# Performer attention and two feed-forward layers: slopes by a sign per feature, five smaller staging buffers, weight units spread over more steps

## The chip, the cores and the metric

The kernel runs on one core of a Trainium2 chip. The metric is the time of one execution on the device in microseconds (us), the median of several runs.

Five engines work beside each other, each in the order of its own instructions, and wait for one another by semaphores: TensorE (PE in the profile; its weight loads are PEld), VectorE (DVE), ScalarE (ACT), GpSimd (POOL) and SyncE (SP), which here only issues transfers (DMA). Products land in PSUM, and DVE or ACT read them from there.

## The reference, cut to what matters

```python
# attention: q, k, v are (4, 8, 576, 64), omega is (128, 64)
h = x @ omega.T - sum(x*x)/2;  phi = exp(h - max(h)) / sqrt(128)      # for scaled q and k
num = phi(q) @ (phi(k).T @ v);  den = phi(q) @ sum(phi(k)) + 1e-6
x = (num / den)                                # as (2304 tokens, 512)
# layer 0 ("moe")
h = x @ w_in                                   # (2304, 2048)
g = np.maximum(h, 0.0) + alpha * np.minimum(h, 0.0)   # one slope alpha per feature, 0 to 0.3
x = g @ w_out                                  # (2304, 512)
# layer 1 ("moe2")
r = np.maximum(x @ w_in2, 0.0)
out = (r * r) @ w_out2
```

All inputs are float32, and so is the output.

## The kernel before

**Numbers in two parts.** TensorE multiplies in a rounded float32 (F32R in the code). Each operand is split: ACT rounds it (the high part), DVE subtracts the rounded from the raw (the low part, the remainder), and a product is three matmuls: high by high, high by low, low by high. `xh`, `xl` are the parts of the inputs, `gh`, `gl` those of the features, and the weights w hold both parts side by side.

**Stages.** Attention comes first (to about 145 us). Then layer 0 runs over three blocks of 768 tokens; in a block, eight turns each take one pair p of feature chunks of 128. Block 0 multiplies plainly (`plain`, eight steps a turn). Blocks 1 and 2 use a scheme of Strassen's kind with seven products of halves (`pair`, seven steps a turn, each one product of six matmuls of 384 columns). In PSUM two tiles a and b collect the products; ACT copies a to s (line 816), and DVE adds s to b (`plus`, line 821), which gives a quarter c of the features. Between the products, TensorE does the second multiplication (`mm2`, line 886) of the pair before, into y, in ten parts handed out by `FILL`. A turn of blocks 1 and 2 has 42 matmuls of products and 48 of `mm2`, 90 in all. At the end of a block y is copied out of PSUM (`evacuate`, line 904).

**The slopes** (`activate`, lines 740 to 762). For each quarter ACT makes n = relu(-c) and r = relu(c); when both halves of a chunk are there, DVE makes r = n * (-alpha) + r over 768 columns (line 754), ACT rounds it to gh (line 757), and DVE takes the remainder gl (line 760). These three are not issued at once: `catch_up` and `round_up` put each a step later on its engine than the one before.

**The weights of layer 1.** The inputs' weights arrive as float32 pairs of words, which have to be put together again: GpSimd loads 128 x 512 of them (512 KB, line 113), ACT scales two words (lines 123, 126), DVE shifts and merges (130, 133), GpSimd adds (135) into the tile `wf1`. DVE then makes four sums of weights (line 149), ACT rounds all eight pieces into staging tiles (line 196), DVE puts the remainders beside them (line 199), and SP writes the tiles to DRAM (`keep`, line 202, and `keep3`, line 223), from where layer 1 reads them later. One such run over 1792 KB of result is a unit; layer 1 has 16 of them (two kinds, `cast1` and `cast3`), made in blocks 1 and 2 of layer 0, eight in each.

**Staging and order.** There are two staging tiles, ma (three pieces, 768 KB) and ms (four pieces, 1024 KB), used by every unit in turn. `plan_unit` (line 287) lays a unit out on ten plan steps: casts into ma at 5 and 7, remainders at 6 and 8, write of ma at 8; casts into ms at 10 and 11, remainders at 11 and 13, write of ms at 13. Line 959 says how far the plan has to be at each of TensorE's 56 steps of a block: in block 1 it is spread over 44 steps from step 5 on, in block 2 over 46 from step 3 on. The work of the plan is issued on ACT, DVE, GpSimd and SP between the work of the steps, and each engine keeps to that order.

**Next block.** `NEXT` (line 403) lists the steps at which the inputs of the next block are prepared: four differences on DVE (line 386), seven roundings on ACT (393) and seven remainders on DVE (396), most of them from step 50 of a block to step 2 of the next.

SP also reads the weights of the next pair from DRAM into a ring of two (line 368): per turn 2 x 896 KB for the products and 2 x 512 KB for `mm2`.

Of the kernel before, what the change touches and what calls it, by code (L numbers as in the profile page):

```python
# [18 lines left out]
P = 128  # L19
# [35 lines left out]
def tile_performer_moe(ctx, tc, qt, kt, qn, kn, vn, omt, w1i, w1o, al, w2i, w2o, out):  # L55
# [8 lines left out]
    al_sb = const.tile([P, NF], F32, name="al_sb")  # L64
    x = const.tile([P, BLOCKS, KC, NB], F32, name="x")
# [90 lines left out]
    def made():  # L156
# [28 lines left out]
        def first(key, u, a0, a1):  # L185

            layer, p = key
            if layer == 0:
                return ring[p % 2][0][:, u, a0:a1]
            return tiles["ma"][:, u, a0 - A22:a1 - A22] if a1 <= S1 else tiles["ms"][:, u, a0 - S1:a1 - S1]  # L190
# [10 lines left out]
        def keep(key, which, at, tile, queue=nc.sync):  # L201
            queue.dma_start(out=kept[key][which][:, :, at].bitcast(F32), in_=tile.bitcast(F32))

            if at in (0, slice(0, 7), slice(3, 7)):
                done.add((key, which))
# [3 lines left out]
        def third(a0, a1):  # L209
            n, a = ("ma", 0) if a1 <= 3 else ("ms", 4)  # L210
            t = tiles[n].rearrange("p u n q -> p (u n q)").rearrange("p (n u q) -> p n u q", u=2, q=QW)
            return t[:, a0 - a:a1 - a]
# [74 lines left out]
        def plan_unit(n, base):  # L287
# [7 lines left out]
            if n1:  # L295
                cast, rest, keeps = (lambda *r: cast1(n1, *r)), (lambda *r: rest1(n1, *r)), [
                    lambda: keep(n1, 0, slice(0, 3), tiles["ma"]), lambda: keep(n1, 0, slice(3, 7), tiles["ms"])]
                first_, second_ = (A11, S1), (A22, A11)
            else:
                cast, rest, keeps = cast3, rest3, [lambda: keep3(n2[1], 0, 3), lambda: keep3(n2[1], 4, 8)]  # L300
                first_, second_ = (0, 2), (2, 3)
            put(-1 if n not in ENDS else 0, lambda: used[n, *a].scale_high())
# [119 lines left out]
    def attention():  # L422
        with ExitStack() as ac:
# [235 lines left out]
            for i in range(NT):  # L659
# [7 lines left out]
                if i == 8:  # L667
                    nc.vector.tensor_scalar(out=al_sb, in0=al_sb, scalar1=-1.0, scalar2=None, op0=ALU.mult)
# [61 lines left out]
    def features(layer, p):  # L730
# [9 lines left out]
        def activate(i, l, c, psum=False):  # L740

            ts = slice(l * HB, (l + 1) * HB)
            f = 2 * p + i
            if i not in halves:
                halves[i] = [new("r", 3, NB), new("n", 2, NB), 0]
            r, n = halves[i][:2]
            halves[i][2] += 1
            nc.scalar.activation(out=n[:, ts], in_=c, func=AF.Relu, scale=-1.0)
            nc.scalar.activation(out=r[:, ts], in_=c, func=AF.Relu)  # L749
            if halves[i][2] < 2:  # L750
                return

            def slope():
# [8 lines left out]
            behind[0].append((slope, high, low))  # L762

        def square(i, l, c, psum=False):

            to = g[i, l, p // 4][:, p % 4]
            if psum:
                r = new("r", 3, NB)[:, :HB]
                nc.scalar.activation(out=r, in_=c, func=AF.Relu)
# [16 lines left out]
            behind[0].append((power, high, low))  # L786

        return gh, gl, square if layer else activate

    def plain(p):  # L790

        w = ring[p % 2][0]
        gh, gl, activate = features(0, p)
# [481 lines left out]
```

## Time and profile before

| | |
|---|---|
| median of 3 runs | 905.99 us (902.18 to 906.78) |
| the profiled execution | 901.07 us, its span 899.0 us |
| granted TensorE clock, mean | 0.997 |
| busy: PE, PEld | 881.9 us (98%), 834.8 us (93%) |
| busy: DVE, ACT, POOL | 673.4 us (75%), 522.6 us (58%), 166.2 us (18%) |
| DMA | 228.81 MB, mean 255 GB/s |

The span runs from the first to the last instruction of the profiled execution. Busy time of a matmul includes its way through the array, so that neighbours overlap; how many matmuls pass in a stretch tells more than PE's busy share. In the lists of instructions a row has the line of the kernel, the engine, the operation, what it writes and reads, its shape and count, then busy time in us and mean ns of one, then the idle time before it and who ended it.

### The profile page before, as it was taken

How to read it: one execution, taken by the hardware profiler on the slowest of the kernel's cores; microseconds unless marked ns; L12 is line 12 of the kernel's file. 1: busy time of each engine (PE TensorE's matmuls, PEld its weight loads, DVE VectorE, ACT ScalarE, POOL GpSimd, SP SyncE). 2: the span in 40 equal slices, each digit the busy share in tenths (PEclk: the TensorE clock that was granted, in tenths of full speed). 3: DMA queues.
4: the chain of work that ended last, by engine and by line, in shares of the span. 5: the costliest groups of instructions: out<-in, count | busy, mean ns of one | idle time of the engine just before them, and what ended most of it. 6: DMA issues, size and time to landing. Idle time of an engine off the chain costs nothing.

```text
span 899.0 us, 18473 instructions
## 1 busy us (share of the span) xinstructions
PE 881.9 (98%) x7328; PEld 834.8 (93%) x7328; DVE 673.4 (75%) x1077; ACT 522.6 (58%) x1109; POOL 166.2 (18%) x192
## 2 busy tenths in 40 slices
PE   9999999999999999999999999999999999999998
PEld 7998889999998888898898999999999999999998
DVE  5868987998986887877788974668855688657674
ACT  6889886777676666667676753334523245333432
POOL 6642322444412322202232100000000000000000
PEclk9999999999999999999999999999999999999999
DMA  7644316898836999927999975767697686876763
GB/s 272 196 139 144 120 30 219 293 303 284 291 141 227 348 399 375 337 92 291 393 348 366 369 266 168 249 249 264 235 309 250 205 322 251 268 259 228 297 249 135
DMA packets 82293, 228.81 MB, mean 255 GB/s; under 512 B 6176, under 2 KB 16800, under 8 KB 77216
## 3 DMA queue, kind: packets, MB, share of 16 engines
q1 hardware_dynamic: 72640, 192.21, 59.7%
q0 software_dynamic: 9216, 33.56, 11.2%
q10 hardware_dynamic: 352, 1.87, 0.6%
q8 instruction: 58, 0.95, 0.4%
q14 instruction: 27, 0.22, 0.1%
HBM read 170.47 MB, written 57.15 MB: 253 GB/s over the span
## 4 chain that ended last, share of the span: by engine, by line
PE 52%; DMA 2%; DVE 2%; ACT 1%; issue 0%; ACTq 0%; DVEq 0%
PE h L717 15%; PE sumb L717 10%; PE suma L1075 9%; PE sumc L1075 8%; PE y L886 7%; PE sumb L1075 3%; DMA k<-ms 2%; DVE r L754 0%; PE h L1075 0%; DVE wf L149 0%; DVE ma L199 0%; ACT x L123 0%; DVE gl L760 0%; DVE c L821 0%; DVE t L130 0%
## 5 line engine op out<-in xcount | busy, mean ns | idle before, releaser
L717 PE MATMUL h<-xh,w 128*128 128x384 f32 x1040 | 296.6, 338 | 6.2 <-ACT s L816 6.2
L717 PEld LDWEIGHTS h<-xh,w 128*128 128x128 f32 x1040 | 191.5, 188 | 10.5 <-ACT s L816 8.0
L886 PE MATMUL y<-gh,w 128*128 128x512 f32 (+1 forms) x768 | 176.9, 339 | 5.2 <-ACT gh L757 5.0
L717 PE MATMUL h<-xl,w 128*128 128x384 f32 x520 | 175.2, 337 | 0.2 <-DVE xl L396 0.2
L886 PEld LDWEIGHTS y<-gh,w 128*128 128x128 f32 x768 | 131.7, 189 | 18.2 <-ACT gh L757 6.8
L135 POOL TENSOR_TENSOR wf<-x 128x512 int32<-128x512 int32 x64 | 81.9, 1280 | 240.5 <-issue 43.5
L1089 ACT CAST gh<-g 128x768 fp32r<-128x768 f32 x72 | 56.6, 833 | 81.0 <-PE suma L1075 38.9
L886 PE MATMUL y<-gl,w 128*128 128x512 f32 (+1 forms) x384 | 103.6, 338 | 0.0
L717 PEld LDWEIGHTS h<-xl,w 128*128 128x128 f32 x520 | 98.0, 188 | 3.2 <-DVE xl L396 0.6
L717 PE MATMUL sumb<-xh,w 128*128 128x384 f32 x336 | 91.2, 335 | 0.0
L1091 DVE TENSOR_TENSOR gl<-g,gh 128x768 fp32r<-128x768 f32 x72 | 65.8, 955 | 32.2 <-PE suma L1075 17.2
L886 PEld LDWEIGHTS y<-gl,w 128*128 128x128 f32 x384 | 67.5, 188 | 9.2
L717 PEld LDWEIGHTS sumb<-xh,w 128*128 128x128 f32 x336 | 61.4, 188 | 0.2 <-ACT s L1021 0.2
L1075 PE MATMUL sumc<-w,gh 128*128 128x256 f32 x416 | 61.3, 283 | 0.0
L499 DVE TENSOR_REDUCE mx<-h 128x8 f32<-128x1024 f32 x36 | 44.0, 1223 | 21.9 <-PE h L486 21.4
L754 DVE SCALAR_TENSOR_TENSOR r<-n,al_sb,r 128x768 f32<-128x768 f32 x48 | 55.9, 1164 | 1.4 <-ACT r L749 1.4
L1075 PEld LDWEIGHTS sumc<-w,gh 128*128 128x128 f32 x416 | 56.5, 192 | 0.0
L717 PE MATMUL sumb<-xl,w 128*128 128x384 f32 x168 | 56.2, 335 | 0.0
L1075 PE MATMUL suma<-w,gh 128*128 128x256 f32 x432 | 54.8, 283 | 0.0
L760 DVE TENSOR_TENSOR gl<-r,gh 128x768 fp32r<-128x768 f32 x48 | 53.4, 1116 | 0.9 <-ACT gh L757 0.9
L1075 PEld LDWEIGHTS suma<-w,gh 128*128 128x128 f32 x432 | 53.1, 192 | 0.0
L821 DVE TENSOR_TENSOR c<-h,s 128x384 f32<-128x384 f32 x51 | 28.2, 553 | 30.6 <-PE h L717 17.8
(112 smaller groups left out, 1554.5 us busy)
## 6 DMA issues: line engine op xcount, KB each, us to landing
w<-k SPq DMA_DIRECT2D x99, 512.0 KB, 5.2
w<-k SPq DMA_DIRECT2D x39, 1024.0 KB, 4.9
w<-k SPq DMA_DIRECT2D x26, 896.0 KB, 9.0
k<-ms SPq DMA_DIRECT2D x16, 1024.0 KB, 7.8
k<-w SPq DMA_DIRECT2D x7, 1792.0 KB, 7.8
k<-ma SPq DMA_DIRECT2D x16, 768.0 KB, 7.0
x<-in_w1i POOLq DMA_DIRECT2D x16, 512.0 KB, 4.1
x<-in_w1o POOLq DMA_DIRECT2D x16, 512.0 KB, 5.3
```

The costliest lines, as they stand in the source:

```text
L135: nc.gpsimd.tensor_tensor(out=self.out.bitcast(I32), in0=self.high, in1=self.low, op=ALU.add)
L499: nc.vector.reduce_max(out=mx, in_=pj, axis=AX.X)
L717: nc.tensor.matmul(out, w[:, u, a, cs], tiles[v, b][:, kc], start=start and kc == 0 and j == 0, stop=stop and kc == 1 and j == 2, skip_gro ...
L754: nc.vector.scalar_tensor_tensor(out=r, in0=n, scalar=al_sb[:, f:f + 1], in1=r, op0=ALU.mult, op1=ALU.add)
L760: nc.vector.tensor_tensor(out=gl[:, i], in0=r, in1=gh[:, i].bitcast(F32), op=ALU.subtract)
L821: nc.vector.tensor_tensor(out=c, in0=b, in1=s, op=ALU.add)
L886: nc.tensor.matmul(y[a0 // 512][:, a0 % 512:a0 % 512 + a1 - a0], u[:, i, c * P:(c + 1) * P], v[:, i, ts], start=first and j == 0 and a0 % ...
L1075: nc.tensor.matmul(to[c], (l if v == 2 else h)[:, r, c * P:(c + 1) * P], w[:, rr, v % 2], start=fresh and rr == 0 and v == 0 and (c != 1 o ...
L1089: nc.scalar.copy(out=h[:, r], in_=f[:, r])
L1091: nc.vector.tensor_tensor(out=l[:, r], in0=f[:, r], in1=h[:, r].bitcast(F32), op=ALU.subtract)
```

## The change

Three things are changed. First, the slopes: a table `sg_sb` holds a sign per feature, -1 where alpha is over 1 and +1 elsewhere. ACT's copy s and the quarter read straight from PSUM are scaled by the sign, DVE's sum becomes b * sign + s in one operation, the slope becomes max(c * alpha, c), and rounding and remainder multiply by the sign again. The relus are gone. In layer 1 the code is arranged anew; its operations stay.

Second, the staging: instead of ma and ms there are a tile for a single piece and a ring of four for two pieces each, the fourth being `wf2`, which is free by then. Each cast takes its own tile (`take`), and each remainder is followed by its own write, four per unit.

Third, line 959 (now 1004) spreads the units over 50 steps in block 1 and 49 in block 2.

```diff
+    sg_sb = const.tile([P, NF], F32, name="sg_sb")
...
+        def take(a0, a1):
+            if a1 - a0 == 1:
+                slots[a0] = tiles["single"]
+            else:
+                slots[a0] = tiles["double"][taken[0] % 4]
+                taken[0] += 1
...
+            def staging(a0, a1):
+                def begin():
+                    take(a0, a1)
+                    cast(a0, a1)
+                def end():
+                    rest(a0, a1)
+                    save(a0, a1)
+                return begin, end
+            (c1, r1), (c2, r2), (c3, r3), (c4, r4) = (staging(*at) for at in (first_, second_, (S1, S3), (S3, 8)))
...
-            put(5, lambda: merge(used[n, *b]), lambda: cast(*first_))
-            put(6, lambda: rest(*first_))
-            put(7, lambda: cast(*second_), lambda: sums((1, 2), not n1))
-            put(8, lambda: rest(*second_), keeps[0])
+            put(5, lambda: merge(used[n, *b]), c1)
+            put(6, r1)
+            put(7, c2, lambda: sums((1, 2), not n1))
+            put(8, r2)
             put(9, lambda: sums((3, 4), not n1))
-            put(10, lambda: cast(S1, S3))
-            put(11, lambda: cast(S3, 8), lambda: rest(S1, S3))
-            put(13, lambda: rest(S3, 8), keeps[1])
+            put(10, c3)
+            put(11, c4, r3)
+            put(13, r4)
...
-                    nc.vector.tensor_scalar(out=al_sb, in0=al_sb, scalar1=-1.0, scalar2=None, op0=ALU.mult)
+                    nc.vector.tensor_scalar(out=sg_sb, in0=al_sb, scalar1=1.0, scalar2=-2.0, op0=ALU.is_gt, op1=ALU.mult)
+                    nc.vector.tensor_scalar(out=sg_sb, in0=sg_sb, scalar1=1.0, scalar2=None, op0=ALU.add)
...
-            nc.scalar.activation(out=n[:, ts], in_=c, func=AF.Relu, scale=-1.0)
-            nc.scalar.activation(out=r[:, ts], in_=c, func=AF.Relu)
...
+            if s is None:
+                scaled(c[:, ts], b, i)
+            else:
+                nc.vector.scalar_tensor_tensor(out=c[:, ts], in0=b, scalar=sign, in1=s, op0=ALU.mult, op1=ALU.add)
...
-                nc.vector.scalar_tensor_tensor(out=r, in0=n, scalar=al_sb[:, f:f + 1], in1=r, op0=ALU.mult, op1=ALU.add)
+                nc.vector.scalar_tensor_tensor(out=c, in0=c, scalar=slope, in1=c, op0=ALU.mult, op1=ALU.max)
...
-                nc.scalar.copy(out=gh[:, i], in_=r)
+                scaled(gh[:, i], c, i)
...
-                nc.vector.tensor_tensor(out=gl[:, i], in0=r, in1=gh[:, i].bitcast(F32), op=ALU.subtract)
+                nc.vector.scalar_tensor_tensor(
+                    out=gl[:, i], in0=c, scalar=sign, in1=gh[:, i].bitcast(F32), op0=ALU.mult, op1=ALU.subtract)
...
-    for n, a in (("ma", 3), ("ms", 4)):
-        tiles[n] = mr.tile([P, 2, a, QW], F32R, name=n)
+    tiles["single"] = mr.tile([P, 2 * QW], F32R, name="ma")
+    tiles["double"] = [mr.tile([P, 4 * QW], F32R, name=f"ms{j}") for j in range(3)]
+    tiles["double"].append(tiles["wf2"].rearrange("p i n -> p (i n)").bitcast(F32R))
...
-                upto(end_of(ENDS[k - 1]) + (end_of(ENDS[k]) - end_of(ENDS[k - 1])) * (turn * 7 + m - (0, 5, 3)[k]) // (0, 44, 46)[k],
+                upto(end_of(ENDS[k - 1]) + (end_of(ENDS[k]) - end_of(ENDS[k - 1])) * (turn * 7 + m - (0, 5, 3)[k]) // (0, 50, 49)[k],
```

On ACT, in the middle of a block, before: the casts into staging (ma, ms), the copies s that TensorE waits for, and the relus n and r.

```order
L196 CAST ma<-wf_98 128x256
L816 COPY s<-h 128x384
L123 ACTIVATE x<-x 128x512
L196 CAST ms<-wf_98 128x512
L126 ACTIVATE x<-x 128x512
L196 CAST ms<-wf_98 128x512
L816 COPY s<-h 128x384
L748 ACTIVATE n<-c 128x384
L749 ACTIVATE r<-c 128x384
```

The same place of a unit on ACT after the change:

```order
L212 CAST ma<-wf_99 128x256
L771 ACTIVATE gh<-c,sg_sb 128x768
L771 ACTIVATE s<-h,sg_sb 128x384
L125 ACTIVATE x<-x 128x512
L212 CAST ms_2690<-wf_99 128x512
L128 ACTIVATE x<-x 128x512
L212 CAST ms_2691<-wf_99 128x512
L771 ACTIVATE s<-h,sg_sb 128x384
L125 ACTIVATE x<-x 128x512
L771 ACTIVATE c<-h,sg_sb 128x384
```

The casts still stand ahead of a copy s, but each has a tile of its own and no relus follow.

On SP's queue, where the first units of block 1 are written (k<-) between the reads of weights (w<-), before:

```order
L202 DMA k_1_0_72<-ma 256x1x768
L368 DMA w_1_2696<-k_5_85 128x2x512
L368 DMA w_0_100<-k_0_4_68 128x1792
L368 DMA w_1_2696<-k_5_85 128x2x512
L202 DMA k_1_0_72<-ms 256x1x1024
```

and after the change:

```order
L218 DMA k_1_0_73<-ms_2689 256x1x512
L218 DMA k_1_0_73<-ma 256x1x256
L396 DMA w_1_2695<-k_5_86 128x2x512
L396 DMA w_0_101<-k_0_4_69 128x1792
L218 DMA k_1_0_73<-ms_2690 256x1x512
L396 DMA w_1_2695<-k_5_86 128x2x512
L218 DMA k_1_0_73<-ms_2691 256x1x512
```

Two writes of a unit became four smaller ones, from four tiles.

On DVE in the last turn of block 1, where the remainders xl of the next block's inputs are made, before:

```order
L821 TENSOR_TENSOR c<-h,s 128x384
L760 TENSOR_TENSOR gl<-r,gh 128x768 x2
L396 TENSOR_TENSOR xl_1358<-x,xh_1357 128x768
L396 TENSOR_TENSOR xl_1360<-x,xh_1359 128x768
L821 TENSOR_TENSOR c<-h,s 128x384
L396 TENSOR_TENSOR xl_2685<-tb,xh_2684 128x768
L396 TENSOR_TENSOR xl_2683<-ta,xh_2682 128x768
```

and after the change:

```order
L795 SCALAR_TENSOR_TENSOR gl<-c,sg_sb,gh 128x768
L135 SCALAR_TENSOR_TENSOR x<-x,t 128x512
L424 TENSOR_TENSOR xl_1360<-x,xh_1359 128x768
L215 TENSOR_TENSOR ms_2689<-wf_99,ms_2689 128x512
L132 TENSOR_SCALAR t<-x 128x512
L424 TENSOR_TENSOR xl_1362<-x,xh_1361 128x768
L784 SCALAR_TENSOR_TENSOR c<-h,sg_sb,s 128x384
L135 SCALAR_TENSOR_TENSOR x<-x,t 128x512
L424 TENSOR_TENSOR xl_2682<-tb,xh_2681 128x768
L215 TENSOR_TENSOR ms_2690<-wf_99,ms_2690 128x2x256
```

Weight work (t, x, ms) now stands between these remainders, where the plan had ended before.

## Rows read from the trace of the kernel before

**Rows 1.** Busy time by stretch: start:end, us, engines (x instructions), PEclk, DMA share, GB/s

```profile
150.00:260.00 110.00, 110.00 (x630) 102.97 (x630) 99.36 (x141) 81.86 (x153) 43.40 (x46) 1.00 0.80 273
270.00:480.00 210.00, 198.63 (x1111) 182.20 (x1110) 162.33 (x263) 142.65 (x282) 50.48 (x56) 0.99 0.85 315
300.00:360.00 60.00, 55.96 (x314) 50.80 (x314) 46.98 (x80) 39.41 (x80) 15.27 (x16) 1.00 1.00 380
380.00:396.00 16.00, 15.69 (x90) 14.36 (x89) 13.07 (x19) 10.42 (x20) 0.30 (x1) 1.00 0.39 132
450.00:455.00 5.00, 5.00 (x23) 4.70 (x22) 4.97 (x8) 3.82 (x8) 1.90 (x2) 0.66 1.02 415
480.00:510.00 30.00, 30.00 (x172) 27.61 (x171) 27.96 (x46) 21.93 (x44) 8.54 (x8) 1.00 0.99 381
```

**Rows 2.** Whom PE waited for, whole span: us in total, times, longest us

```profile
PE h L717 <- ACT s L816: 6.2, 5, 1.7
PE y L886 <- ACT gh L757: 5.0, 4, 2.0
PE t L480 <- DVE pick L455: 1.2, 1, 1.2
PE h L486 <- ACT e L511: 0.4, 1, 0.4
PE h L717 <- DVE xl L396: 0.2, 1, 0.2
```

**Rows 3.** Timeline of ACT and PE, 372 to 376: start, us, instruction, [idle before, releaser]

```profile
372.75 0.62 ACT L196 CAST ms<-wf 128x512 fp32r<-128x512 f32 x1 [3.54 <-DMA k<-ms]
...
374.87 0.45 PE L717 MATMUL h<-xh,w 128*128 128x384 f32 x1 [1.59 <-ACT s L816]
```

**Rows 4.** Who waited for whom, all engines, whole span

```profile
ACT ms L196 <- DMA k<-ms: 17.1, 7, 4.0
```

**Rows 5.** Timeline of PE behind the start of block 2

```profile
415.50 0.96 PE L886 MATMUL y<-gh,w 128*128 128x512 f32 x4 [0.84 <-ACT gh L757]
```

**Rows 6.** DMA issues: count, KB each, median us from issue to landing

```profile
k<-ms SPq DMA_DIRECT2D x16, 1024.0 KB, 7.8
...
k<-ma SPq DMA_DIRECT2D x16, 768.0 KB, 7.0
```

**Rows 7.** Instructions of ACT, 276 to 545 us

```profile
L757 ACT CAST gh<-r 128x768 fp32r<-128x768 f32 x32 | 26.7, 833 | 1.8 <-DVE r L754 1.6
...
L748 ACT ACTIVATE n<-c 128x384 f32<-128x384 f32 x46 | 24.2, 526 | 33.9 <-DVE c L821 33.9
...
L816 ACT COPY s<-h 128x384 f32<-128x384 f32 x48 | 22.7, 473 | 9.6 <-PE h L717 9.1
```

**Rows 8.** Instructions of ACT by shape, to 276 and from 276 us

```profile
L511 ACT ACTIVATE e<-h,nb 128x128 f32<-128x128 f32 x144 | 39.1, 384 | 13.0 <-DVE nb L506 13.0
...
L904 ACT COPY x<-y 128x256 f32<-128x256 f32 x4 | 1.5, 372 | 0.6 <-DVE x L904 0.6
```

**Rows 9.** Instructions of DVE, 276 to 545 us

```profile
L754 DVE SCALAR_TENSOR_TENSOR r<-n,al_sb,r 128x768 f32<-128x768 f32 x32 | 34.2, 1068 | 0.0
L760 DVE TENSOR_TENSOR gl<-r,gh 128x768 fp32r<-128x768 f32 x32 | 33.1, 1040 | 0.0
L821 DVE TENSOR_TENSOR c<-h,s 128x384 f32<-128x384 f32 x49 | 27.1, 554 | 29.7 <-PE h L717 17.8 <-ACT s L816 11.5
...
L199 DVE TENSOR_TENSOR ms<-wf,ms 128x512 fp32r<-128x512 f32 x32 | 26.1, 816 | 12.2 <-ACT ms L196 12.2
L149 DVE TENSOR_TENSOR wf<-wf 128x256 f32<-128x256 f32 x64 | 25.5, 419 | 2.4 <-POOL wf L135 1.9
...
L133 DVE SCALAR_TENSOR_TENSOR x<-x,t 128x512 int32<-128x512 int32 x32 | 22.0, 687 | 0.3
L199 DVE TENSOR_TENSOR ma<-wf,ma 128x512 fp32r<-128x512 f32 (+1 forms) x32 | 21.8, 681 | 8.5 <-ACT ma L196 8.5
...
L130 DVE TENSOR_SCALAR t<-x 128x512 int32<-128x512 int32 x32 | 14.6, 456 | 5.5 <-ACT x L123 5.3
```

More of the change, by code (lines that the diff above doesn't have):

```diff
@@ L738, in features, with scaled, activate, bend @@
             parts(p)
[L740 removed]
+        def scaled(to, of, i):
+            nc.scalar.mul(out=to, in_=of, mul=sg_sb[:, 2 * p + i:2 * p + i + 1])
+        def activate(i, l, b, s=None):
             ts = slice(l * HB, (l + 1) * HB)
[L743 removed]
+            sign, slope = (t[:, 2 * p + i:2 * p + i + 1] for t in (sg_sb, al_sb))
             if i not in halves:
[L745 to L754 removed]
+                halves[i] = [new("c", 4, NB), 0]
+            c = halves[i][0]
+            halves[i][1] += 1
+            if s is None:
+                scaled(c[:, ts], b, i)
+            else:
+                nc.vector.scalar_tensor_tensor(out=c[:, ts], in0=b, scalar=sign, in1=s, op0=ALU.mult, op1=ALU.add)
+            if halves[i][1] < 2:
+                return None
+            def bend():
+                nc.vector.scalar_tensor_tensor(out=c, in0=c, scalar=slope, in1=c, op0=ALU.mult, op1=ALU.max)
@@ L766, in square, with plain_copy @@
+            return bend, high, low
+        def plain_copy(to, of, i):
+            nc.scalar.copy(out=to, in_=of)
+        def square(i, l, b, s=None):
             to = g[i, l, p // 4][:, p % 4]
+            c = new("c", 4, NB)[:, :HB]
+            psum = s is None
             if psum:
-                r = new("r", 3, NB)[:, :HB]
-                nc.scalar.activation(out=r, in_=c, func=AF.Relu)
+                r = c
+                nc.scalar.activation(out=r, in_=b, func=AF.Relu)
+            else:
+                nc.vector.tensor_tensor(out=c, in0=b, in1=s, op=ALU.add)
@@ L784, in low @@
                                             op=ALU.subtract)
-            behind[0].append((power, high, low))
-        return gh, gl, square if layer else activate
+            return power, high, low
+        return (gh, gl, square, plain_copy) if layer else (gh, gl, activate, scaled)
     def plain(p):
         w = ring[p % 2][0]
-        gh, gl, activate = features(0, p)
+        gh, gl, activate, _ = features(0, p)
         for n, (i, l) in enumerate(((1, 0), (0, 0), (1, 1), (0, 1))):
@@ L806, in pair @@
         w = ring[p % 2][0]
-        gh, gl, activate = features(layer, p)
+        gh, gl, activate, moved = features(layer, p)
         a, b = (mp["ph"].tile([P, 512], F32, name="h")[:, :HB] for _ in range(2))
@@ L812, in product, with copied @@
             multiply(out, w, *PRODUCTS[n], start, True)
-        def copied():
+        def copied(i):
             s = new("s", 2)
-            nc.scalar.copy(out=s, in_=a)
+            moved(s, a, i)
             return s
-        def plus(s):
-            c = new("c", 3)
-            nc.vector.tensor_tensor(out=c, in0=b, in1=s, op=ALU.add)
-            return c
         product(a, 1, True)
-        s = copied()
+        s = copied(0)
         catch_up()
@@ L828, in pair @@
         product(b, 2, True)
-        c = plus(s)
+        one = activate(0, 0, b, s)
         catch_up()
-        activate(0, 0, c)
+        then(one)
         yield
         product(a, 6)
-        s6 = copied()
+        s6 = copied(0)
         catch_up()
@@ L840, in pair @@
         product(a, 7)
-        s7 = copied()
-        c = plus(s7)
+        s7 = copied(1)
+        one = activate(1, 1, b, s7)
         catch_up()
-        activate(1, 1, c)
+        then(one)
         yield
@@ L847, in pair @@
         catch_up()
-        activate(1, 0, a, True)
+        then(activate(1, 0, a))
         yield
         product(b, 3)
-        c = plus(s6)
+        one = activate(0, 1, b, s6)
         catch_up()
-        activate(0, 1, c)
+        then(one)
         yield gh, gl
@@ L866, in catch_up, with then @@
         behind[:] = [], made_, rounded
+    def then(one):
+        if one:
+            behind[0].append(one)
     def round_up():
@@ L1021, in copied @@
             nc.scalar.copy(out=kept_[n], in_=a)
-        def plus(n):
-            c = new("c", 3)
-            nc.vector.tensor_tensor(out=c, in0=b, in1=kept_[n], op=ALU.add)
-            return c
         def step(n):
@@ L1033, in step @@
                 copied(n)
-            c = plus({2: 1, 7: 7, 3: 6}[n]) if n in (2, 7, 3) else None
+            at = {2: (0, 0, 1), 7: (1, 1, 7), 3: (0, 1, 6)}.get(n)
+            one = activate(*at[:2], b, kept_[at[2]]) if at else None
             if n != 3:
                 catch_up()
-            if n == 4:
-                activate(1, 0, a, True)
-            elif c is not None:
-                activate(*{2: (0, 0), 7: (1, 1), 3: (0, 1)}[n], c)
+            then(activate(1, 0, a) if n == 4 else one)
             if p + 2 < NPAIR and n in GROUPS:
```

23 lines of the change are left out of this document (11 added, 12 removed).

## The prediction

> **What bounds the kernel now.** I read the stage windows first, then who waits for whom, then the instruction lists around the waits. TensorE is busy nearly everywhere; the reader is to see where it is not. In block 0 of layer 0 it has no gap [rows 1], and at the end of block 2 it passes 172 matmuls in 30 us, 5.73 per us, so that a turn of 90 matmuls takes 15.7 us. From 270 to 480 us, which is blocks 1 and 2 with the making of layer 1's weights, there are 1111 matmuls in 210 us; at 5.73 they would take 194 us. By busy time the loss there is 11.4 us, and the 5 us with 23 matmuls at a granted clock of 0.66 (a mix of the 1.2 and 2.4 GHz levels, right behind the longest wait of 2.0 us) add about 1 us. I take 14 us as the loss, between 12.4 and 16. The waits say who it is: TensorE waits for ACT alone, 6.2 us for the copy s and 5.0 us for the rounding gh [rows 2]. ACT is late for a reason of its own: its cast into the staging tile ms stood 3.54 us until an earlier write out of ms had landed, the copy s was queued behind it (the order shown with the change), and TensorE stood 1.59 us for s [rows 3]. There are six such waits of TensorE from 304 to 477 us, 1.2 to 2.0 us each, 9.2 us together. ACT's waits for ms are 17.1 us in all [rows 4]. The remaining 2 us are of the kind of [rows 5]: at the start of a block ACT is simply behind, and gh comes 0.84 us late.
>
> **Deeper staging, slower weight plan.** A unit is 10 plan steps. In block 1 eight units lie on 44 of the 56 TensorE steps now, so that a unit takes 5.5 steps of 2.24 us, 12.3 us. Its write out of ms is issued at plan step 13 and the next unit casts into ms at 20: 7/10 of 12.3, 8.6 us, while such a write takes 7.8 us to land [rows 6]. Hardly any slack; that is the wait. After the change a unit takes 50/8 = 6.25 steps, 14.0 us. The small tile is reused after 9 plan steps (12.6 us), the four double ones in turn after 10, 12 or 14 (14.0 us and more), and they land no later than the whole tiles did, as far as their size tells. Slack grows from under 1 us to 5 or 6 us. So the cast no longer waits: 12 us of the 14 go (the 9.2 us, the slow-clock stretch behind them and their part of what the busy time does not show). Bounds: 5 us, if DMA keeps the pace (first rival), and 12.
>
> **Relus out, sign in.** ACT per turn: now three copies of 0.473, eight relus of about 0.526 and two roundings of 0.833 [rows 7], 7.3 us. After: three copies, one scaled read and two roundings, each with a scale read per partition. No row has such a scale, the nearest is the exponential with a bias per partition, 384 ns for 128 columns, where copies of 256 and 384 columns (372 and 473) extrapolate to 271 [rows 8]: 0.11 us dearer. So 3 x 0.58 + 0.58 + 2 x 0.94 = 4.2 us, 3.1 us less per turn; bounds of the surcharge 0 and 0.2, at which it is 3.6 and 2.7. Nearly all of this lies beside TensorE and is worth nothing; it shortens what stands before gh and s where ACT is behind. I take 1 us of the 2 (bounds 0 and 2). Each s and gh itself comes 0.11 us later, which costs nothing while their queue is shorter by two relus.
>
> DVE per turn: three sums of 0.554, two slopes of 1.068, two remainders of 1.040 [rows 9], 5.88 us. All seven become three-operand forms with a scalar per partition, as the slope is already: remainders 1.068, sums 0.55 (half the slope's 768 columns is 0.53; upper end 1.07, if PSUM as a source doubles it). 5.9 us. One hop falls away: a sum no longer goes to ACT and back before the slope. In block 0 four operations per turn change; DVE is busy 99.4 of 110 us there [rows 1] and TensorE has no gap, so 0.03 us each costs nothing. The two tiny operations on the signs lie in attention. Layer 1 gets other tile names, the same operations in the same order. The 34 more writes are issued on SP's queue, whose reads of the next pair are asked for most of a turn ahead.
>
> **What is late next.** The weight work costs DVE 47.9 + 25.5 + 22.0 + 14.6 = 110 us for 16 units [rows 9], 6.9 us each. At 1.12 units per turn that is 7.7 us, with 5.9 it is 13.6 of 15.7 us: 87%, less than now per turn (1.27 units, 14.6). But block 1's plan now runs on through its last turn, where the operands of the next block are made. That turn had 13.1 us of DVE work in 16 us [rows 1], the last unit's tail of some 2 us included; 11 + 7.7 = 18.7 us does not fit into 15.7. DVE falls 3 us behind; the rounding gh that the next turn needs first has 1.6 us of slack (from product 4 to that use TensorE has 36 matmuls, 6.3 us; the last sum must wait for 12 of them, 2.1 us, and sum, slope and rounding then take 0.55 + 1.07 + 0.94). I take 2 us of new stall at the turn from block 1 to 2 (bounds 0 and 4). In block 2 the plan ends after step 52 and the overload is half as large; that is inside the bound.
>
> **The sum**: -12 - 1 + 2 and 1.5 us for waits that the crowded DMA still makes (bounds 0 and 5) = -9.5 us. The profiled execution took 901.1 us (span 899.0): 891.6. The median of the runs is 906.0, 5 us above it; the prediction is made against the median: **896.5 us**.
>
> **Rivals.** *DMA keeps the pace.* From 300 to 360 us DMA is at a share of 1.00 with 380 GB/s [rows 1]. A turn reads 2 x 896 + 2 x 512 KB, a unit writes 1792 and loads 1024 KB, 2816 KB each way. Now 1.273 units per turn are 6.55 MB, at 380 GB/s 17.2 us, and 314 matmuls in 60 us are just 17.2 us per turn: this pace is what TensorE runs at there. After: 1.12 and 1.143 units, 6.11 and 6.18 MB, 16.1 and 16.3 us per turn, so 0.4 x 7.1 + 0.6 x 7 = 7 us stay lost if nothing buffers. Then the staging is worth 5 us, not 12, and with -1 and +2 it is 906.0 - 4 = 902. Against it: the lag of 3 to 4 us per block is less than the slack of 5 to 6 us, it is made good in the free stretch after each plan (share 0.39 from 380 to 396 us), and 415 GB/s were moved from 450 to 455 us. Chance 0.18.
>
> *The block end costs more.* If DVE's 3 us of lag show in full at both block ends and pull the reads along that SP issues behind DVE's remainders, the new stall is 6 us instead of 2 and the time 901. For it speaks the order at the last turn, against it that block 0 runs at 90% of DVE without a gap. Chance 0.10.
>
> *The wait only moves.* With the casts free the remainders, or the reads queued between four writes instead of two, hold TensorE just as long: 905. Against it: none of TensorE's waits is for a read of w [rows 2]. Chance 0.07.
>
> *Slower: DVE becomes the pace.* Place: every turn of blocks 1 and 2. If the seven forms cost 0.5 us more each, DVE needs 13.6 + 3.5 = 17.1 us for a turn of 15.7, and 15 turns lose 21 us where 14 are lost now; block 0, with four such operations and 1.6 us free per turn, loses 3 more: 916. It decides from 0.3 us per operation, and becomes slower by over 0.5% from 0.47. Against it: slope and remainder differ by 0.03 us. Chance 0.04.
>
> *Slower: more and smaller writes.* From 768 to 1024 KB the landing grows by 0.8 us, 7.0 to 7.8 [rows 6], so a straight line leaves 4.6 us that do not depend on size. If these were time of the DMA engines, two more writes per unit would be 9.2 us, 16 units 147 us, and most of it would show: about 1020. Against it: some ten transfers per turn would then need 46 us where a turn takes 17.2. It is delay, not use. Chance 0.01. The Trainium skill, page "DMA: Bandwidth & Descriptors", section Bandwidth, tells one to batch DMAs to 1 MiB or more, which this change goes against; its fit of 2.0 us plus size by 436 GB/s gives, as an estimate, 12.2 instead of 8.2 us for a unit's writes one after the other, 64 us for 16 units. The trace doesn't bear that out as engine time, since 380 GB/s flowed with writes of 768 KB and reads of 512 KB side by side.
>
> **How the numbers follow.** The forecast, 893 to 900 us, has 0.60. 0.5%, about what a measurement of this kernel can tell from no change, is 4.5 us: the bounds are 901.5 and 910.5. Faster: 0.60, half of the first rival, 0.06 of the second, 0.01 of the third, 0.76. Same: 0.09 + 0.04 + 0.06 = 0.19. Slower: 0.05. The range is 889 to 903: it takes in the first two rivals, and below, that the runs 5 us above the profiled one lose still more to the same waits. Outside are the third rival, the slower ones and 0.07 on both ends.
>
> **What would show it.** Right: from 270 to the end of block 2 TensorE's idle time falls from 11.4 us to 2 or 4; ACT's wait for a write out of ms is under 2 us instead of 17.1; layer 1 starts about 10 us earlier; the clock has no stretch under 0.9 there; a stall of 1 to 3 us stands near the start of block 2, ended by ACT's gh with DVE behind it. DMA pace: the share is 1.00 for tens of us and casts still wait for k<-ms. DVE pace: sums of 0.9 us or more. Wrong altogether would be matmuls per us under 5.4 in blocks 1 and 2.

## The result and the profile after

The changed kernel took **892.5 us** (median of 4 runs, 888.29 to 893.57) against 906.32 us (4 runs, 902.18 to 906.78) of the kernel before beside it: a ratio of 0.984, with a 95% interval from 0.980 to 0.988. The gain is 13.8 us where 9.5 was forecast. The time lies inside the range of 889 to 903 us, and 0.5 us below the inner one of 893 to 900.

The profiled execution took 893.57 us, its span is 891.8 us. Busy time of the engines (us, share of the span, instructions):

```profile
PE 881.9 (99%) x7328; PEld 837.0 (94%) x7328; DVE 676.5 (76%) x1078; ACT 480.4 (54%) x965; POOL 169.7 (19%) x192
```

The stretches, with the columns of [rows 1] (busy us and instructions of PE, PEld, DVE, ACT, POOL, then granted clock, DMA share, GB/s):

```profile
150.00:260.00 110.00, 110.00 (x629) 103.14 (x629) 102.31 (x142) 79.01 (x131) 44.53 (x47) 1.00 0.81 273
270.00:480.00 210.00, 208.13 (x1185) 192.60 (x1184) 173.25 (x277) 122.20 (x207) 54.90 (x57) 1.00 0.87 326
300.00:360.00 60.00, 60.00 (x345) 55.96 (x344) 49.94 (x80) 33.99 (x58) 17.09 (x18) 1.00 1.01 380
380.00:396.00 16.00, 16.00 (x94) 14.94 (x93) 15.97 (x25) 11.38 (x19) 4.97 (x2) 1.00 0.44 163
480.00:510.00 30.00, 30.00 (x173) 27.87 (x172) 25.32 (x42) 16.38 (x29) 7.53 (x8) 1.00 1.02 383
```

From 270 to 480 us TensorE's idle time fell from 11.4 to 1.9 us and it passes 1185 matmuls instead of 1111; from 300 to 360 us it has no gap. Whom TensorE waited for (us in total, times, longest):

```profile
PE h L514 <- ACT e L539: 3.3, 3, 2.9
PE y L930 <- ACT gh L771: 1.4, 3, 0.9
PE t L508 <- DVE pick L483: 1.2, 1, 1.2
PE h L746 <- DVE xl L424: 0.3, 1, 0.3
```

The only wait for a write out of a staging tile that is left:

```profile
ACT ma L212 <- DMA k<-ma: 1.7, 1, 1.7
```

The kernel before had 17.1 us of such waits for ms [rows 4] and these for ma:

```profile
ACT ma L196 <- DMA k<-ma: 4.9, 4, 2.4
```

The wait for s, 6.2 us in [rows 2], is gone; that for gh fell from 5.0 to 1.4 us. The 3.3 us at the top lie in attention and are no part of the change: e3 below, whose attention is that of the kernel before, has 3.7 us of them (last section). The operations after, 276 to 533 us (busy us, mean ns of one, idle before), answer to [rows 7] and [rows 9]:

```profile
L795 DVE SCALAR_TENSOR_TENSOR gl<-c,sg_sb,gh 128x768 fp32r<-128x768 f32 x32 | 35.7, 1119 | 0.0
L789 DVE SCALAR_TENSOR_TENSOR c<-c,al_sb 128x768 f32<-128x768 f32 x32 | 34.7, 1085 | 0.0
L771 ACT ACTIVATE gh<-c,sg_sb 128x768 fp32r<-128x768 f32 x32 | 30.0, 938 | 21.1 <-DVE c L789 21.0
L784 DVE SCALAR_TENSOR_TENSOR c<-h,sg_sb,s 128x384 f32<-128x384 f32 x47 | 28.9, 615 | 24.1 <-PE h L746 20.7 <-ACT s L771 2.6 <-ACT ms L212 0.5
L771 ACT ACTIVATE s<-h,sg_sb 128x384 f32<-128x384 f32 x46 | 26.7, 581 | 14.3 <-PE h L746 14.0
```

**A measure of the stage.** The profiled executions differ by up to 13 us in how late they get through attention and block 0 (last section), so spans alone mislead: the two profiles differ by 7.2 us, the medians by 13.8. I compare the time from the first to the last copy of y into x that DVE makes, from the first turn of block 1 to the first turn of layer 1. It is in the row of these copies ("278.0 to 545.9"). Without any stall it would be 16 turns of 15.74 us, 252 us; 15.74 us is the time between the same matmul of two neighbouring turns of e5 (below), at 311.19 and 326.93 us, with no gap between them. Before and after:

```profile
L904 DVE COPY x<-y x12: 411/548/681, 278.0 to 545.9; 128x256 f32<-128x256 f32 x6, 128x512 f32<-128x512 f32 x6
```

```profile
L948 DVE COPY x<-y x12: 415/550/684, 284.2 to 539.2; 128x256 f32<-128x256 f32 x6, 128x512 f32<-128x512 f32 x6
```

That is 267.9 us before and 255.0 after: 12.9 us less, and 3 us over the floor are left.

### The profile page after: what moved, and what is told of

The parts are those of the page before. It is cut to its first block, busy times and chain, and to the rows that moved or that the text cites. A ratio compares the mean times of both kernels' runs of the same rounds, so it can differ in the third digit from the quotient of the medians.

```text
span 891.8 us, 18473 instructions
## 1 busy us (share of the span) xinstructions
PE 881.9 (99%) x7328; PEld 837.0 (94%) x7328; DVE 676.5 (76%) x1078; ACT 480.4 (54%) x965; POOL 169.7 (19%) x192
## 4 chain that ended last, share of the span: by engine, by line
PE 54%; DVE 2%; ACT 0%; issue 0%; DVEq 0%; ACTq 0%
PE h L746 16%; PE sumb L746 10%; PE suma L1113 9%; PE sumc L1113 8%; PE y L930 8%; PE sumb L1113 3%; DVE xl L424 1%; PE h L1113 0%; DVE c L789 0%; DVE ms L215 0%; DVE c L784 0%; DVE wf L151 0%; DVE ta L414 0%; ACT gh L771 0%; DVE gl L795 0%
## 5 line engine op out<-in xcount | busy, mean ns | idle before, releaser
L137 POOL TENSOR_TENSOR wf<-x 128x512 int32<-128x512 int32 x64 | 86.2, 1347 | 240.7 <-issue 56.8
L771 ACT ACTIVATE gh<-c,sg_sb 128x768 fp32r<-128x768 f32 x48 | 45.0, 938 | 38.0 <-DVE c L789 37.9
L789 DVE SCALAR_TENSOR_TENSOR c<-c,al_sb 128x768 f32<-128x768 f32 x48 | 56.4, 1174 | 1.6 <-ACT c L771 1.6
L795 DVE SCALAR_TENSOR_TENSOR gl<-c,sg_sb,gh 128x768 fp32r<-128x768 f32 x48 | 56.6, 1181 | 1.0 <-ACT gh L771 1.0
L771 ACT ACTIVATE c<-h,sg_sb 128x384 f32<-128x384 f32 x48 | 27.8, 580 | 52.0 <-PE h L746 51.6
```

The source lines that it names most:

```text
L137: nc.gpsimd.tensor_tensor(out=self.out.bitcast(I32), in0=self.high, in1=self.low, op=ALU.add)
L771: nc.scalar.mul(out=to, in_=of, mul=sg_sb[:, 2 * p + i:2 * p + i + 1])
L789: nc.vector.scalar_tensor_tensor(out=c, in0=c, scalar=slope, in1=c, op0=ALU.mult, op1=ALU.max)
L795: nc.vector.scalar_tensor_tensor(out=gl[:, i], in0=c, scalar=sign, in1=gh[:, i].bitcast(F32), op0=ALU.mult, op1=ALU.subtract)
```

## The experiments

Theory (A in the expectations): TensorE lost its time because ACT, which works in order, stood at a cast until an earlier write had left the staging tile; own tiles for each write end that, and the plan and the signs add little. Rivals: the slower plan is what helps, since it gives the old tiles time; or the signs, since ACT has less to do (C); or DMA sets the pace whatever the tiles (B). The edits are called the signs (`sg_sb` and all that uses it), the staging (tiles and `take`) and the plan (line 1004). "Stage" below is the measure just told, from one profile each. Each ratio is against runs of the kernel before made beside that kernel: medians of 906.3 us for the change, 905.5 for e1 to e4, 906.9 for e5 to e8, 906.0 for e9 to e11.

| kernel | median us | ratio (95%) | stage us |
|---|---|---|---|
| after: signs, staging, plan | 892.5 | 0.984 (0.980 to 0.988) | 255.0 |
| e1: signs | 906.1 | 1.003 (1.000 to 1.006) | 272.2 |
| e2: staging | 892.3 | 0.986 (0.984 to 0.989) | 254.5 |
| e3: plan | 896.6 | 0.990 (0.986 to 0.994) | 258.9 |
| e4: staging, plan | 893.4 | 0.989 (0.983 to 0.995) | 256.7 |
| e5: signs, staging | 891.3 | 0.984 (0.979 to 0.990) | 254.5 |
| e6: staging with three tiles | 895.4 | 0.988 (0.985 to 0.991) | 256.6 |
| e7: after, more work on DVE | 904.4 | 0.998 (0.994 to 1.001) | 266.9 |
| e8: signs, staging, faster plan | 899.0 | 0.992 (0.988 to 0.997) | 265.4 |
| e9: after, first cast later | 886.6 | 0.978 (0.972 to 0.984) | 255.2 |
| e10: before, first cast later | 901.4 | 0.994 (0.991 to 0.997) | 270.7 |
| e11: signs, staging, first cast later | 886.3 | 0.978 (0.972 to 0.983) | 254.3 |

How far one profile of the stage can be trusted is seen where the same code of the stage was profiled twice: 267.9 and 270.7 us with the old tiles (before, e10), 255.0 and 255.2 (after, e9), 254.5 and 254.3 (e5, e11). With the old tiles a difference of 3 us says little.

### One part at a time

**e1_signs_only.** The kernel before with the signs alone:

```diff
-            nc.scalar.activation(out=n[:, ts], in_=c, func=AF.Relu, scale=-1.0)
-            nc.scalar.activation(out=r[:, ts], in_=c, func=AF.Relu)
...
+                nc.vector.scalar_tensor_tensor(out=c[:, ts], in0=b, scalar=sign, in1=s, op0=ALU.mult, op1=ALU.add)
```

> The slopes by sign alone; two staging tiles and the plan over 44 and 46 steps as before. If the waits for staging tiles make the loss (theory A), ACT still stands behind k<-ms for 15 us or more, and only its shorter queue helps: 1 to 3 us less than before, 903 to 905. If DMA's rate makes it (theory B): no change, 906. If ACT's load of relus makes it (theory C): 8 us or more less, under 898, and the waits of TensorE for s and gh fall to half.

906.1 us: no gain, where theory A had 903 to 905. The time alone is what the DMA rival expected (906); the waits for ms are as theory A had them, and e2 decides. ACT is busy 113.6 us from 270 to 480 us where it was 142.7 [rows 1], but it stands longer at the same writes: 27.0 us for ms and 12.1 for ma, 39 instead of 22 (24 in e10, the kernel before with another attention). Waits of e1:

```profile
ACT ms L198 <- DMA k<-ms: 27.0, 8, 6.4
ACT ma L198 <- DMA k<-ma: 12.1, 4, 3.9
```

The longest of them, with what was queued behind it (start, us, instruction, idle before and releaser), and the stretch behind it in the columns of the stretches:

```profile
475.27 0.62 ACT L198 CAST ms<-wf 128x512 fp32r<-128x512 f32 x1 [6.44 <-DMA k<-ms]
...
476.96 0.69 PE L720 MATMUL h<-xh,w 128*128 128x384 f32 x1 [5.04 <-ACT s L745]
```

```profile
475.00:480.00 5.00, 3.04 (x10) 3.04 (x11) 2.42 (x4) 2.85 (x6) 1.09 (x1) 0.50 0.48 189
```

This is the chain of [rows 3], longer: the cast stands 6.4 us, the copy s behind it, TensorE 5.0 us for s, and then the granted clock is 0.50. A lighter ACT is no cure for a wait at the head of its queue.

**e2_staging_only.** The staging alone, with relus and the old plan:

```diff
-            return tiles["ma"][:, u, a0 - A22:a1 - A22] if a1 <= S1 else tiles["ms"][:, u, a0 - S1:a1 - S1]
+            return staged(a0, a1)[:, u]
...
+                slots[a0] = tiles["double"][taken[0] % 4]
```

> The five smaller staging tiles with four writes per unit alone; relus and the plan over 44 and 46 steps as before. Theory A: ACT's waits for a write fall from 17 to under 5 us; what is left is that DMA is asked for 6.55 MB per turn, so 899 to 903. Theory B: casts, or reads of w, still wait, since the rate is what it was: 905. Theory C: no change, 906.

892.3 us, a stage of 254.5: **the staging alone brings all of the gain**. All three expected times were too long; my 899 to 903 allowed for a limit of DMA that did not show. No engine waits for a write out of a staging tile at all. Its stretches:

```profile
270.00:480.00 210.00, 208.07 (x1183) 192.54 (x1182) 175.03 (x281) 152.60 (x301) 53.77 (x59) 1.00 0.88 332
300.00:360.00 60.00, 60.00 (x343) 55.75 (x342) 51.97 (x86) 43.92 (x88) 18.54 (x21) 1.00 1.02 399
380.00:396.00 16.00, 16.00 (x93) 14.90 (x92) 12.72 (x18) 11.11 (x20) 0.55 (x1) 1.00 0.25 78
```

ACT still carries the relus and is busy 152.6 us from 270 to 480 us, and TensorE has no gap from 300 to 360 us, with 399 GB/s flowing. So 380 GB/s was what the waits left of DMA, not its ceiling.

**e3_plan_only.** Line 959 alone:

```diff
-                upto(end_of(ENDS[k - 1]) + (end_of(ENDS[k]) - end_of(ENDS[k - 1])) * (turn * 7 + m - (0, 5, 3)[k]) // (0, 44, 46)[k],
+                upto(end_of(ENDS[k - 1]) + (end_of(ENDS[k]) - end_of(ENDS[k - 1])) * (turn * 7 + m - (0, 5, 3)[k]) // (0, 50, 49)[k],
```

> The plan over 50 and 49 steps alone; relus and two staging tiles as before. Reuse of ms then comes 9.8 us after its write is issued instead of 8.6, and DMA is asked for 6.11 MB per turn. Theory A: the waits shrink but don't go, 899 to 903, with ACT's wait for k<-ms at 5 to 10 us. Theory B: the rate fits, 896 or less. Theory C: 906, or more, as relus, weight work and the next block's operands meet in the last turn of block 1.

896.6 us, a stage of 258.9: 9.0 of the 13.4 us that the staging takes off it (8.9 of 13.2 by the medians). Theory A had 899 to 903; the time comes closer to the DMA rival's 896, which e2 excludes. The old tiles get more time between uses; casts still wait, but seldom long enough to reach TensorE:

```profile
ACT ms L196 <- DMA k<-ms: 10.7, 5, 4.2
ACT ma L196 <- DMA k<-ma: 5.2, 3, 2.3
```

Waits of TensorE in the same run, for [rows 2]:

```profile
PE y L886 <- ACT gh L757: 2.2, 3, 0.8
PE h L717 <- ACT s L816: 1.7, 4, 0.8
```

Before, 22.0 us of waits on ACT stood beside 11.2 us on TensorE; now 15.9 stand beside 3.9. Of these 3.9 us, some 3.2 stand in e4 too, where no cast waits: 0.84 us at the start of each block and 0.80, 0.55 and 0.22 at the end of block 1. So the waits of casts that are left cost TensorE some 0.7 us. The rival holds for the plan on its own, and yet the plan and the staging don't add, since they remove the same wait: on top of the plan the staging takes 2.2 us off the stage (e4), by itself 13.4.

### What the parts do together

**e4_staging_and_plan.** The changed kernel without the signs:

```diff
-                nc.vector.scalar_tensor_tensor(out=c[:, ts], in0=b, scalar=sign, in1=s, op0=ALU.mult, op1=ALU.add)
...
+            nc.scalar.activation(out=n[:, ts], in_=c, func=AF.Relu, scale=-1.0)
+            nc.scalar.activation(out=r[:, ts], in_=c, func=AF.Relu)
```

> Staging tiles and plan together, relus as before: the change without its signs. Theory A: 894 to 897, no wait for a write, and the waits that are left are ACT's at the block ends. Theory B: as with the plan alone, 896. Theory C: 904 or more.

893.4 us, a stage of 256.7: 2.2 us longer than with the staging alone. There is no wait for a write. Three stalls that e2 does not have stand at the end of block 1, where the plan now runs on: 0.80, 0.53 and 0.22 us, 1.55 of the 2.2. The stretch, and the two longest of them:

```profile
380.00:396.00 16.00, 14.67 (x82) 13.07 (x81) 15.60 (x24) 12.26 (x24) 3.17 (x2) 1.00 0.34 126
```

```profile
383.36 0.44 PE L743 MATMUL h<-xh,w 128*128 128x384 f32 x1 [0.80 <-ACT s L842]
...
395.71 0.97 PE L912 MATMUL y<-gh,w 128*128 128x512 f32 x4 [0.53 <-ACT gh L783]
```

DVE is busy 15.6 of 16 us where it was 12.7 in e2, and TensorE passes 82 matmuls instead of 93, which are some 1.9 us of its time. This is the overload that the prediction worked out, with its 2 us, but it is one of ACT as well as of DVE. At the second stall ACT had stood 2.68 us for DVE's sum before it came to the relus and gh. At the first, the longer one, the copy s starts at 382.84 us behind relus, weight casts and a rounding xh for block 2, and ACT has had no idle time since 379.67 us.

**e5_no_plan.** The changed kernel with the old plan, `(0, 44, 46)`.

> The change without its plan: signs and staging, units over 44 and 46 steps as before. If the staging alone made the gain and the wider plan only adds a crowd at the block ends (theory A2, from the run with staging alone), 890 to 893, no longer than the change, with one stall of under 1 us at the start of a block and none at 380 to 400 us. If the signs only pay where the plan is wide (they make room at the block ends), and the plan pays with them (theory P), 894 to 897.

891.3 us, a stage of 254.5, as e2. So the signs are worth nothing with the old plan (254.5 with or without) and 1.7 us with the new one (256.7 to 255.0), where they ease the last turn; and the new plan is worth nothing once the staging is there: it costs 0.5 us with the signs and 2.2 without. That e5 equals e2 hides two small things: at the start of block 1 TensorE waits 0.29 us for gh in e5 and 0.84 in e2, and in e5 it waits 0.44 us for a read of w, which it does not in e2. From 300 to 360 us of e5:

```profile
300.00:360.00 60.00, 60.00 (x345) 55.90 (x344) 51.55 (x87) 35.84 (x62) 19.35 (x20) 1.00 1.03 407
```

**e6_staging_three_deep.** e2 with a ring of three double tiles, so that the staging takes 1792 KB as before, only cut finer:

```diff
-                slots[a0] = tiles["double"][taken[0] % 4]
+                slots[a0] = tiles["double"][taken[0] % 3]
```

> Staging alone as before, but a ring of three double tiles instead of four: the same 1792 KB of staging as the two tiles had, only cut finer, each piece written as soon as it is complete. Reuse comes after 8 or 9 plan steps, 9.8 to 11.1 us, instead of 8.6. If the finer cut is what removes the wait (landing 6.8 us, so 3 us of slack are enough): 892 to 894, ACT's waits for writes under 3 us. If the fourth tile's depth is needed: 896 to 900, with waits of ACT of 5 us and more.

895.4 us, between the two answers that I had expected, and so are ACT's 4.1 us of waits. A stage of 256.6: 11.3 of the 13.4 us come with no byte more, from cutting the tiles so that each write frees its own, which also puts off reuse from 7 plan steps to 8 or 9. The fourth tile brings the last 2.1 us. TensorE waits for gh four times, 3.7 us in all, the longest time here:

```profile
ACT ms L210 <- DMA k<-ms: 4.1, 5, 1.5
```

```profile
357.52 0.95 PE L912 MATMUL y<-gh,w 128*128 128x512 f32 x4 [1.32 <-ACT gh L783]
```

### The edges: DVE and DMA

**e7_more_dve.** The changed kernel, with each remainder of blocks 1 and 2 computed twice: 32 more operations, 2.24 us of DVE per turn:

```diff
+                for _ in range(times):
+                    nc.vector.scalar_tensor_tensor(
+                        out=gl[:, i], in0=c, scalar=sign, in1=gh[:, i].bitcast(F32), op0=ALU.mult, op1=ALU.subtract)
...
-        gh, gl, activate, moved = features(layer, p)
+        gh, gl, activate, moved = features(layer, p, 2)
```

> The change with the remainder gl computed twice in blocks 1 and 2 (the same values again): 2 x 1.12 us more on DVE per turn, 32 operations, 36 us in all. By the step 'DVE becomes the pace': 13.7 + 2.2 = 15.9 us per turn against 15.7, so 3 us over the plan's turns and 2 to 4 us more at the block ends, 897 to 900. If DVE in truth has room (its idle time can be moved): 893. If its order makes every extra operation count (each delays a sum or a slope that TensorE waits for): 905 and more.

904.4 us, a stage of 266.9: 11.9 us for 36 us of work, and a miss for my 897 to 900. The added work, then the stretch, then whom TensorE waited for in these blocks:

```profile
L796 DVE SCALAR_TENSOR_TENSOR gl<-c,sg_sb,gh 128x768 fp32r<-128x768 f32 x64 | 69.6, 1089 | 1.1
```

```profile
270.00:480.00 210.00, 200.65 (x1128) 183.15 (x1126) 190.72 (x286) 114.63 (x195) 49.76 (x55) 1.00 0.84 309
```

```profile
PE h L746 <- ACT s L771: 4.1, 5, 1.8
...
PE h L746 <- DVE c L784: 2.5, 3, 1.5
PE y L931 <- ACT gh L771: 2.1, 4, 0.9
PE h L746 <- DVE xl L424: 1.3, 1, 1.3
```

DVE is busy 91% of the stretch and TensorE already stands 9.35 us. The arithmetic by turns had it that 13.7 + 2.2 = 15.9 us is barely over 15.7. In the middle of block 1 it did fit:

```profile
300.00:360.00 60.00, 60.00 (x345) 55.86 (x344) 55.80 (x86) 33.19 (x56) 15.21 (x16) 1.00 1.01 381
```

DVE is busy 93% there and TensorE has no gap. Of some 10 us of stalls in the two blocks 5.4 lie from 382 to 421 us, where the operands of block 2 are made as well. So the added work costs most where a block ends, more there than the 2 to 4 us that I had allowed for the block ends. Why DVE can't use more of the time that is free was not tested.

**e8_fast_plan.** The changed kernel with a plan faster than before, `(0, 38, 40)`, which asks more of DMA per turn:

> Signs and staging with the units over only 38 and 40 steps: 1.47 and 1.40 units per turn, 7.13 and 6.92 MB per 15.7 us, 454 and 441 GB/s. If DMA has a ceiling near the 415 GB/s of its best stretches, turns take 17.2 and 16.7 us there, 8 and 6 us lost in all less what the tiles buffer (4 to 6 us per block): 897 to 905, and casts wait for k<-ms again. If rate is no limit here: 893.

899.0 us, inside the 897 to 905 expected of a ceiling of DMA, and a stage of 265.4. Its stretch, the waits and the longest stall:

```profile
300.00:360.00 60.00, 55.30 (x305) 50.71 (x304) 50.31 (x90) 35.82 (x64) 18.73 (x19) 0.97 1.04 407
```

```profile
ACT ma L212 <- DMA k<-ma: 9.1, 4, 4.3
PE h L746 <- DMA w<-k: 7.0, 4, 3.5
```

```profile
349.18 0.61 PE L746 MATMUL h<-xh,w 128*128 128x384 f32 x2 [3.48 <-DMA w<-k]
```

As in e5 407 GB/s flow, but 305 matmuls pass instead of 345: TensorE now waits for the reads of w, a wait that no other kernel has at this size. The casts wait for ma rather than for ms, which I had expected. Ahead of the longest stall, from 325 to 350 us, the reads of w of 896 KB land after 13.2 us at the median, beside 9.6 in e5, while no more bytes move (409 GB/s in e8, 413 in e5).

I read this as a ceiling of DMA at about 407 GB/s over 60 us (5 us of e8 reach 420), with e5 just below it (a single stall of 0.4 us for w); that the order on SP's queue has a part in the stalls is not excluded. If so, the slower plan has a use that the times don't show: it gives back room, 380 GB/s over the same stretch of the changed kernel.

### The first cast in attention

The median of the kernel before lies 5 us above its profile, and the two profiles differ by less than the medians. Both go back, in the main, to one place, ahead of what the change gains from. `MAKE_K` sets the step of attention from which weight work is mixed in; in these runs it is 3 instead of 2:

```diff
-MAKE_K = 2
+MAKE_K = 3
```

**e9_later_first_cast** has this in the changed kernel, **e10_before_later_first_cast** in the one before, **e11_no_plan_later_first_cast** in e5.

> The change, with the first weight work in attention one step later (MAKE_K 3 instead of 2): ACT's first scaling of loaded weights then stands behind 24 exponentials instead of 16. If ACT's wait for that load (2.9 us in the change's profile, 3.7 in another, not there in the one of before) and the half clock behind it make the 4 to 12 us by which runs of one kernel differ: 886 to 889, granted clock 0.998 or more, and runs that spread by less than 3 us. If the clock falls there for another reason: 892, spread as before.

> The kernel before with the same one step. If the late load belongs to both kernels alike, and so was neither gain nor loss of the change: 898 to 901, and the distance to the change with that step stays 12 to 14 us. If before was not touched by it: 905.

> Signs and staging, units over 44 and 46 steps, and the first weight work one step later: the version that the runs so far point to. 885 to 888, within 1 us of the change with the same step, since the plan is worth nothing beside the staging; 3 us or more longer if the plan does pay once attention no longer blurs the time.

e9 took 886.6 us and its four runs lie within 0.5 us (886.40 to 886.89); e11 took 886.3 (884.93 to 886.57). Both beat both kernels. The kernel before gains some 5 us as well (901.4, against 898 to 901 expected), but its runs still spread by 6 us (897.68 to 903.76). Its one profile has 1.0 us of stall left in attention, and beside it the waits of the old staging, which I take for the rest of the spread without having shown it:

```profile
ACT ms L196 <- DMA k<-ms: 19.2, 7, 5.2
PE h L717 <- ACT s L816: 7.7, 5, 3.3
```

With the first cast later in both, the change is worth 901.4 - 886.6 = 14.8 us (12 to 14 expected), and 11.3 between the quickest runs of either. Between e9 and e11, with and without the new plan, there are 0.3 us: nothing.

## Why the prediction was right

**The bound.** As read from [rows 2 to 4]: casts that stand for a write, s and gh behind them in ACT's order, TensorE behind those. e1, e2 and e6 show it from three sides: a lighter ACT leaves the loss, own tiles end it, and a finer cut of the same bytes ends most of it. Of the prediction's own signs these came: 1.9 us of idle time on TensorE where it had 2 or 4, no wait for ms, no lower clock in these blocks. Layer 1 starts 6.7 us earlier in the profile and not 10, since block 1 starts 6.2 us later there.

**Staging and plan, -12 us.** Measured 13.4 us less in the stage for the staging alone, 12.9 for all of the change (-13.4, 0 for the signs, +0.5 for the plan). What was mis-sized is the loss: of the 12.4 to 16 us that [rows 1] gave I took 14, the middle. Against the floor of the stage it was 267.9 - 252 = 16, the upper end, which the count of matmuls had given; the busy time shows less than is lost. The 2 us that I let stay, and a little more, did stay. Why it works was told as one thing in two parts, slower plan and deeper tiles; the runs part them: the tiles are enough, the plan alone gives 9.0 us, and on top of the tiles it gives nothing. That I had not said.

**Signs, -1 us.** ACT's prices were right: s 581 ns (0.58 taken), gh 938 (0.94). DVE's were somewhat low: sums 615 (0.55), slopes 1085 and remainders 1119 (1068), 6.25 us per turn instead of 5.9. ACT is busy 20.5 us less from 270 to 480 us. The worth was 0 with the old plan and 1.7 us beside the new one: inside the bounds, and for the reason given, that ACT counts only where it is behind.

**The last turn, +2 us.** The place was right and so was the crowd on DVE, which is busy 15.97 of 16 us from 380 to 396 us; the crowd on ACT, which makes the longest stall of e4, was not in it. Without the signs it costs 2.2 us (e4), with them 0.5. The stalls there are 0.25 us, 0.30 (for xl) and 0.88, the last of which answers to [rows 5]:

```profile
397.43 0.97 PE L930 MATMUL y<-gh,w 128*128 128x512 f32 x4 [0.25 <-ACT gh L771]
...
414.99 0.97 PE L930 MATMUL y<-gh,w 128*128 128x512 f32 x4 [0.88 <-ACT gh L771]
```

My 2 us left out that the signs, whose worth stood in another term, ease this very turn.

**Waits of the crowded DMA, +1.5 us.** None was seen. With 1.4 us too little for the staging and 1.5 too much for the last turn, this is one of three terms of about the same size that made the forecast too small; that no worth of the signs showed by itself took 1 us back. In the changed kernel TensorE waits for no read of w, and ACT for one write, 1.7 us at 443 us, behind which TensorE has no stall. It came from the first rival's ceiling of 380 GB/s, at a share of 1.00 in [rows 1]. 399 and 407 GB/s flow in e2 and e5 without a stall: a share of 1.00 said that the engines were occupied, not that they could move no more. The DMA issues of the changed kernel (count, KB each, median us to landing):

```profile
k<-ms SPq DMA_DIRECT2D x36, 512.0 KB, 6.8
...
k<-wf SPq DMA_DIRECT2D x12, 512.0 KB, 8.1
...
k<-ma SPq DMA_DIRECT2D x16, 256.0 KB, 7.2
```

A third of the size lands no sooner than 768 KB did, 7.0 us [rows 6], and half of 1024 KB, which took 7.8, at 6.8 or 8.1. Yet 64 writes instead of 32 (32 more, not the prediction's 34) cost nothing, as the last rival's counter-argument had it: this is delay, not use. The Trainium skill's page "DMA: Bandwidth & Descriptors", section Bandwidth, which advises transfers of 1 MiB or more, would have spoken for the kernel before; here the kernel with the smaller writes is 13 us faster (e2), since what counts is when a tile comes free. The fit that the prediction took from this page is one for DMAs that GpSimd issues; these writes are issued by SP.

**The other rivals.** The wait did not move (e2, after). That DVE becomes the pace was rightly put at a small chance, but its edge lies nearer than I had it: e7 loses 12 us at 2.24 us more per turn, 0.32 us for each of the seven forms, where the prediction's rule ("decides from 0.3") had a loss only begin.

**The base.** The prediction was made 5 us above the profile, at the median. That was right, and its reason is in the last section. Against the profile the same sum gives 891.6 us, which would have met 892.5 by luck, with 9.5 us of gain where 13.8 was measured. The gain also depends on which runs are compared. Where the whole run was granted a clock of 1.0, the kernel before took 898.85 us at best and the changed one 888.29: 10.6 us. The other runs have lower mean clocks, those of before more so, and I can't part what of that attention and what staging caused in runs that have no profile.

**Left open.** That the signs alone lengthened the waits by 17 us is read from one profile, and why they did was not tested. The signs and the plan without the staging were not run together. The stall at the start of block 2 stood in before, after, e2 and e4 to e6 (0.83 to 0.88 us), and nothing here removed it.

## What to carry to other kernels

A cast into a tile that is still being written out stops all that stands behind it on its in-order engine; look first whether the tile can be cut so that each write frees its own, before spreading the work or making the engine lighter. Parts of a change that remove the same wait don't add up: price each on top of the others, and where one is enough, ask what the other costs. Where runs scatter by more than the effect, compare a stage, from one landmark to another, and look for what scatters.

## What the runs showed of the hardware

**A short stall in attention can cost more than three times its length, and makes much of the scatter of the runs.** There ACT's first scaling of weights waits for its load, and TensorE for the exponential behind it. In the changed kernel:

```profile
15.86 0.67 ACT L125 ACTIVATE x<-x 128x512 f32<-128x512 f32 x1 [2.92 <-DMA x<-in_w1i]
```

```profile
18.65 1.81 PE L514 MATMUL h<-om,raw 64*128 64x128 f32 x16 [2.90 <-ACT e L539]
```

Behind these 2.9 us of idle time the granted clock is 0.50, the lower of its two levels (1.2 GHz), and TensorE passes 70 matmuls in 5 us:

```profile
20.00:25.00 5.00, 5.00 (x70) 4.61 (x66) 2.50 (x4) 4.46 (x15) 2.63 (x3) 0.50 0.18 62
```

The same stretch of the profile of before, where ACT does not wait for this load:

```profile
20.00:25.00 5.00, 5.00 (x126) 4.60 (x124) 4.41 (x8) 4.53 (x17) 4.38 (x5) 1.00 0.50 161
```

The stage begins at 284.2 us in the changed kernel instead of 278.0, 6.2 us later. In e6, with a stall of 3.7 us, the clock is 0.50 from 20 to 40 us, and the stage begins at 290.4, 12.4 us later. In e5, with a stall of 1.8 us, the clock stays at 1.00 and the stage begins at 279.1, only 1.1 us later. The time of a run goes with its mean clock: e6 took 889.04 us at 1.0 and 902.16 at 0.987. One step later for the first cast, in e9, ACT does not wait for the load, and the runs agree within 0.5 us.

**DMA's share of 1.00 is not its limit** (from 300 to 360 us): 380 GB/s at 1.00 before, 407 GB/s at 1.03 in e5 without a stall, and 407 at 1.04 in e8 with stalls of up to 3.5 us.
